# Fused attention and FFN: scratch weights stored by product and four features, half as many block moves, and a re-spaced plan

## The chip, the cores and the metric

The kernel runs on one core of a Trainium2 chip. The metric is the device time of one execution in microseconds. Engines: PE (matmul), PEld (its weight loads), DVE (vector), ACT (scalar), POOL (GpSimd), and SP, whose queue issues every DMA of this kernel.

## What is computed

Eight batches of 576 tokens; 8 heads of width 64. Heads 0 to 3 attend to the last 32 positions, heads 4 to 7 to every fourth of the last 128. The heads' outputs, put side by side, are the rows of x (4608 x 512), and a feed-forward layer follows:

```python
scores = np.where(masks[None], scale * np.matmul(q, k.transpose(0, 1, 3, 2)), -1e9)
attn = np.exp(scores - np.max(scores, -1, keepdims=True))
attn = attn / (np.sum(attn, -1, keepdims=True) + 1e-09)
x = np.matmul(attn, v)                     # then heads side by side: 4608 x 512
h = x @ w_in                               # 512 -> 2048
g = 0.5 * h * (1.0 + erf(h / sqrt(2)))
out = g @ w_out                            # 2048 -> 512
```

All in float32. A float32 operand of a large matmul is kept as a high and a low part of type fp32r, and a block takes three matmuls (high by high, low by high, high by low).

## The kernel before

**Tiling.** The 4608 tokens are nine chunks of 512; chunk 8 gathers the last 64 tokens of every batch. The eight heads of a chunk are four pairs p, treated two at a time as duos (p = 0 and p = 2). The feed-forward width is 16 features f of 128.

**Stages.** Chunks 0, 1 and 2 are computed densely: 192 matmuls of 128x128 by 128x512 for the hidden layer, 192 for the output. Chunks 3 to 8 go in three chunk pairs (`two_chunks`, line 1192), each layer as a two-by-two block product in seven products P1 to P7 (Winograd's form of Strassen), 672 matmuls a chunk pair. A *unit* is one product of one of eight features: six matmuls. The order of the units of a layer is a list: `first_units` (line 867), `second_units` (line 874).

**Scratch weights.** The products need sums of weight blocks. `prepare(layer, f, due)` (line 889), 16 calls in all, makes them while chunks 1 and 2 are computed: POOL adds high and low parts (line 906, two instructions), DVE forms four sums (line 914), ACT writes their high parts (line 926), DVE the low ones (line 929), and SP stores them to DRAM (`put`, line 931: four DMAs; `plain`, line 909: three DMAs straight from the weights). A unit's weights stand in `slabs` in the order of the unit list, four units of 1 MB a slab. `fetch` (line 1200) loads a slab into one of five ring tiles. Two unit tiles (`prep`) allow two preparations in flight.

**Attention beside it.** `attend` (line 1008) does a duo: a *scores visit* on PE (line 448), masked scores and minima on DVE, 16 exponentials on ACT (line 496), scaling and a transposition in 32x32 blocks on DVE (`turn`, line 523), moves of the turned blocks between partitions (`move`, line 1000), and a *values visit* on PE (line 577) for which the values v_sb must be loaded too. A duo's head pair takes eight moves of 32 KB:

```python
for r in range(4):
    for j in range(2):
        to = r // 2 * 2 + j
        nc.sync.dma_start(s.t[32 * to:32 * to + 32, r % 2], half[32 * r:32 * r + 32, j])
```

**Order of the work.** `Flow` (line 166) is a planner that runs when the program is built: jobs have an engine, a guessed time, due times and pool slots, and the planner fixes the order of the instructions of every engine; on the chip each engine and SP's queue works through its list in that order and waits where a semaphore says so. `pe` (line 825) puts a visit between matmuls when its time in PE's own clock has come, at least `VISITS` apart; the table `duos` (line 1435) holds those times, and `prepare` gets its due times in the loop at line 1450. Pools limit what may be in flight: 19 tiles of 1 MB (`w`), of which weights hold 16 until chunk 2 has used them, six PSUM banks for matmuls, two for visits, and three small tiles `go` for the hidden layer after gelu and for output copies.

Of the kernel before, what the change touches and what calls it, by code (L numbers as in the profile page):

```python
# [19 lines left out]
P = 128  # L20
# [145 lines left out]
class Flow:  # L166
# [4 lines left out]
    def __init__(self):  # L171
        self.busy, self.units, self.held, self.jobs, self.table = {}, {}, {}, [], ""

    def add(self, engine, time, do=None, after=(), due=0.0, begin=0.0, take=(), give=(), table="", land=0.0):
        j = dict(engine=engine, time=time, do=do, after=list(after), due=due, begin=begin, take=list(take), give=list(give),
                 table=table, land=land, ready=0.0, then=[])
        self.jobs.append(j)
        return j
# [15 lines left out]
    def run(self):  # L194
# [7 lines left out]
        while there:  # L202
# [14 lines left out]
            end = at + j["time"]  # L217
            self.table = j["table"] or self.table
            if e:
                self.busy[e] = end  # L220
            end += j["land"]
# [16 lines left out]
        assert n == len(self.jobs), (list(self.held), [(j["engine"], j["due"], j["take"]) for j in there if j["engine"] != "DMA"])  # L238
# [13 lines left out]
def attn_ffn(ctx: ExitStack, tc: tile.TileContext, qk, qk_lp, qk_ld, v, v_ld, w, outT):  # L252
# [270 lines left out]
    def turn(s):  # L523
        if s.wide:
            s.t = []
            for h in range(2):
                yield {"DVE": 0.5}
                t = work.tile([P, 3 * NU, KB], F32, tag="sm", name="turned", bufs=7)
                nc.vector.transpose(t.rearrange("p i b -> p (i b)"), s.sm[h].rearrange("p u k -> p (u k)"))
                s.t.append(t)  # L530
            return
        yield {"DVE": 0.62}
        s.t = work.tile([P, 2, 2 * NU, KB], F32, tag="sm", name="halves", bufs=7)
        nc.vector.transpose(s.t.rearrange("p j i b -> p i j b"), s.all.rearrange("p i (j b) -> p i j b", j=2))
# [303 lines left out]
    VISITS, WIDE_STEP, EXP_DUE = 5.0, 9.0, 5.0  # L838
# [28 lines left out]
    first_units = []  # L867
    for s in range(HALF):
        first_units += [(u, s - i) for i, u in enumerate((P1, P6, P7, P4)) if s >= i]
    first_units += [(P6, 7), (P7, 6), (P4, 5), (P5, 0), (P7, 7), (P4, 6), (P2, 0), (P5, 1), (P4, 7), (P2, 1), (P3, 0)]  # L870
    for f in range(2, HALF):
        first_units += [(P5, f), (P2, f), (P3, f - 1)]
    first_units.append((P3, HALF - 1))
# [3 lines left out]
    NSLAB = len(first_units) // 4  # L877
    place = [{u: i for i, u in enumerate(units)} for units in (first_units, second_units)]
    slabs = [scratch.tile([P, 4, 2, NW1], F32, name=f"slab{i}", tag=f"slab{i}") for i in range(2 * NSLAB)]

    def slab_at(layer, u, f):
        i = place[layer][u, f]
        return slabs[layer * NSLAB + i // 4][:, i % 4]

# [4 lines left out]
    def prepare(layer, f, due):  # L889
# [3 lines left out]
        names = (B11, B21, B12, B22) if layer == 0 else (B11, B12, B21, B22)  # L893
        at = {x: i for i, x in enumerate(names)}
        key = ("prepare", layer, f)
        cols = slice(layer * DM, (layer + 1) * DM)
        y = lambda x: st["q"][:, at[x], 1].bitcast(F32)
        weight = lambda x: weights[f if at[x] < 2 else g][:, :, layer * DM + at[x] % 2 * NW1:layer * DM + (at[x] % 2 + 1) * NW1]

        def add_up(i):  # L900
            def go():
                if i == 0:
                    st["q"] = wpool.tile([P, 4, 2, NW1], F32R, tag="w", name="units")
                x = weights[g if i else f].bitcast(F32)
                a, b = (x[:, k, cols].rearrange("p (i k) -> p i k", i=2) for k in range(2))
                nc.gpsimd.tensor_add(st["q"][:, 2 * i:2 * i + 2, 1].bitcast(F32), a, b)  # L906
# [12 lines left out]
        away = [flow.add("DMA", 2.0, plain, due=due, begin=due - 12, land=2.0)]  # L919
# [16 lines left out]
        away.append(flow.add("DMA", 2.7, put, [j], due + 1, land=2.0, give=[key]))  # L936
# [63 lines left out]
    def move(s):  # L1000

        half, s.t = s.t, work.tile([P, 2, 2 * NU, KB], F32, tag="sm", name="turned", bufs=7)
        for r in range(4):
            for j in range(2):
                to = r // 2 * 2 + j
                nc.sync.dma_start(s.t[32 * to:32 * to + 32, r % 2], half[32 * r:32 * r + 32, j])  # L1006

    def attend(c, p, scores_at, exps_at, values_at, lead=(14, 15)):
# [8 lines left out]
        def softmax_of(i, o, after, at, e):  # L1017
# [14 lines left out]
            else:  # L1032
                half = ("half",) + kk
                j = chain("DVE", [0.71], turn(o), [norms[-1]], e + 6 + 4 * step, step, take=[("sm", half)], give=[("sm",) + kk + (0,)])
                turns = [flow.add("DMA", 1.0, lambda: move(o), j, e + 6 + 5 * step, 0.0, turned, [half], land=2.2)]
# [3 lines left out]
        if wide:  # L1039
            for i, o in enumerate(pairs):  # L1040
                key = ("qk", c, o.p)
                q = flow.add("DMA", 2.6, load_qk(o, 1), due=scores_at[i] - 5, begin=scores_at[i] - lead[0], take=[("w", key)], land=2.0)
# [7 lines left out]
        else:  # L1050
            if c > 2:
                n = 2 if s.rest else 1
                keys = [("w", ("qk", c, p) + (i,) * i) for i in range(n)]
                q = [flow.add("DMA", 3.2 if s.rest else 2.6, load_qk(s, n), due=scores_at[0] - 5, begin=scores_at[0] - lead[0], take=keys, land=2.0)]
# [12 lines left out]
        if not wide:  # L1067
            key = ("v", c, p)
            vs = flow.add("DMA", 2.6, load_values(s), due=values_at - 6, begin=values_at - lead[1], take=[("w", key)], land=2.0)
# [26 lines left out]
        more = [("more", c, i) for i in range(2)]  # L1096
# [3 lines left out]
        for i, o in enumerate(pairs):  # L1100
            key = ("v", c, o.p)
            vs = flow.add("DMA", 2.0, load_values(o), due=values_at - 6 + i, begin=values_at - lead[1], take=[("w", key)], land=2.0)

            def run(o=o):
# [5 lines left out]
            def out(o=o):  # L1110
                c0 = o.p % 2 * P
                at_once(put_x(o, [ps[:, m, c0:c0 + P] for m in [6, 7] + [bank_of(x) for x in more]]))
            visit = flow.add("PE", 2.0, run, [turned[i], vs] + ([] if i else [turned[1]]),
                             take=[("upper", up)] + [("bank", x) for x in more] if not i else [],
                             give=[key] + [("turned", c, o.p, h) for h in range(2)])
            if i:
                visit["after"].append(puts[-1]["after"][0])
            visits.append((values_at + WIDE_STEP * i, visit))
            puts.append(flow.add("ACT", 1.7, out, [visit] + there[:1], values_at + WIDE_STEP * i + 4,
                                 take=[] if there else [("w", ("x",) + kx)]))  # L1120
            there.append(puts[-1])
        meet(puts, [up] + more)
# [23 lines left out]
    def chunk(c, parts):  # L1146
# [33 lines left out]
        for d in range(NC):  # L1180
# [7 lines left out]
            flow.add("DMA", 0.7, store, [k], clock[0] + 4 + d, give=[("o", c, d)], land=2.0)  # L1188
# [3 lines left out]
    def two_chunks(n):  # L1192
# [7 lines left out]
        def fetch(layer, i):  # L1200
            key = ("slab", n, layer, i)
# [3 lines left out]
            def go():  # L1205
                made[key] = wpool.tile([P, 4, 2, NW1], F32R, tag="w", name="ring")
                nc.sync.dma_start(made[key].rearrange("p m t k -> p (m t k)").bitcast(F32),
                                  slabs[layer * NSLAB + i].rearrange("p m t k -> p (m t k)"))
            units = (first_units, second_units)[layer][4 * i:4 * i + 4]
            after = {id(a): a for u, f in units for a in put_in[layer, u, f]}.values() if n == 0 else []  # L1210
            fetched[key] = flow.add("DMA", 2.6, go, list(after), clock[0] - 8, clock[0] - 25,
                                    take=[("w", key), ("ring", ("r",) + key)], land=2.0)
            return fetched[key]

        def weight(layer, u, f):
            i = place[layer][u, f]
            return (lambda: made["slab", n, layer, i // 4][:, i % 4]), fetch(layer, i // 4), \
                [("slab", n, layer, i // 4), ("r", "slab", n, layer, i // 4)] if i % 4 == 3 else []
# [119 lines left out]
        def keep_acc(name, bank, due, after=(), give=()):  # L1338

            jobs = []  # L1340
            for d in range(2):
# [4 lines left out]
                jobs.append(flow.add(("ACT", "DVE"), 0.6, go, [last[0]] + jobs + list(after), due + d, take=[("xg", ("acc", n, name))] if d == 0 else [],  # L1346
# [3 lines left out]
        def finish(name, bank, i, j, after, due, give=True, n_parts=1):  # L1350

            jobs, stores = [], []
            for d in range(2):
                for m in range(n_parts):
# [11 lines left out]
                    stores.append(flow.add("DMA", 0.7 / n_parts, store, [x], due + 2 + d, land=2.0))  # L1366
# [3 lines left out]
        evac2 = {}  # L1370
        for q, (u, f) in enumerate(second_units):
# [27 lines left out]
            def mm(u=u, f=f, w=w, b=b, begins=begins, key=key, ds=(0, 1)):  # L1399
# [6 lines left out]
            pe(6 * MM, mm, [got, second[u, f]] + before,  # L1406
               [("bank", (n, b, d)) for d in range(2)] if begins and f == 0 else [], slab_give + [key])
# [9 lines left out]
            elif u == P7:  # L1417
                j = keep_acc("u3", b, t)
                k = finish("p4", b, 1, 0, [last[0]] + evac2[P4], t + 1, give=False)
                meet(j + k, [(n, b, d) for d in range(2)])  # L1420
                evac2[P5] = finish("u3", "b", 1, 1, j, t, give=False)
            elif u == P2:
                finish("c1", b, 0, 0, [last[0]] + evac2[P1], t + 1)
            elif u == P3:
                finish("u2", b, 0, 1, [last[0]] + evac2[P6], t + 1, n_parts=2 if n == NPAIRS - 1 else 1)
# [3 lines left out]
    def visit_times(c, p, scores_at, exps_at, values_at, *more):  # L1429
# [5 lines left out]
    duos = [(2, 0, 2, (22.5, 27.5), 60), (2, 2, 8, (31, 36), 68), (3, 0, 14, (66, 71), CH + 6, (9, 12)),  # L1435
            (3, 2, 72, (75, 80), CH + 13, (9, 12)), (4, 0, CH + 18, (CH + 22.5, CH + 27.5), CH + 50, (9, 12)),
            (4, 2, CH + 24, (CH + 31, CH + 36), CH + 57, (9, 12))]
    for n in range(NPAIRS - 1):
        t, c = 2 * CH + n * PAIR, 5 + 2 * n
        duos += [(c, 0, t - 30, (t - 25, t - 20), t + 8), (c, 2, t + 1, (t + 3, t + 8), t + 22),  # L1440
                 (c + 1, 0, t + 10, (t + 13, t + 18), t + 36),
                 (c + 1, 2, t + 20, (t + 23, t + 28), t + 50) if c + 1 < LAST else
                 (c + 1, 2, (t + 18, t + 26), (t + 21, t + 29), t + 48)]
# [110 lines left out]
```

## Time and profile before

| | us |
|---|---|
| runs shown | 895.88 median of 3 (894.19 to 904.04) |
| the profiled execution | 896.98, of which the span of its instructions is 895.2 |
| granted TensorE clock, mean | 0.963 of full speed |
| busy | PE 837.5, PEld 688.4, DVE 596.3, ACT 469.7, POOL 56.5 |

A stretch of the trace is named by its start and end in microseconds. Chunk 0 with its weight loads runs to 136.7, chunks 1 and 2 to 383.6, the two chunk pairs with attention beside them to 662.6 (first layer of the second pair ended), the rest to 890.6, and the last additions and stores end at 895.2. Of each engine the rows give busy time, of SP the time that issuing took (SPq). A bracket behind an instruction is the idle time just before it on its engine and what ended it.

### The profile page before, as it was taken

How to read it: one execution, taken by the hardware profiler on the slowest of the kernel's cores; microseconds unless marked ns; L12 is line 12 of the kernel's file. 1: busy time of each engine (PE TensorE's matmuls, PEld its weight loads, DVE VectorE, ACT ScalarE, POOL GpSimd, SP SyncE). 2: the span in 40 equal slices, each digit the busy share in tenths (PEclk: the TensorE clock that was granted, in tenths of full speed). 3: DMA queues.
4: the chain of work that ended last, by engine and by line, in shares of the span. 5: the costliest groups of instructions: out<-in, count | busy, mean ns of one | idle time of the engine just before them, and what ended most of it. 6: DMA issues, size and time to landing. Idle time of an engine off the chain costs nothing.

```text
span 895.2 us, 19887 instructions
## 1 busy us (share of the span) xinstructions
PE 837.5 (94%) x8115; PEld 688.4 (77%) x8115; DVE 596.3 (67%) x950; ACT 469.7 (52%) x1187; POOL 56.5 (6%) x77
## 2 busy tenths in 40 slices
PE   7899999967886898998999999999899999999998
PEld 5778888846765786887888888787788888888886
DVE  6896977754874151657579677685597774389664
ACT  6786834552634263546565446555554443465441
POOL 5000012323240000000000000000000000000000
PEclk9799999988997898999999999899999999999999
DMA  9956127868977416276787546786855259655202
GB/s 372 416 219 266 48 94 250 273 203 245 328 233 223 180 32 252 93 268 218 247 348 293 191 182 230 239 297 236 349 203 199 98 199 386 261 192 194 85 0 95
DMA packets 60717, 195.55 MB, mean 218 GB/s; under 512 B 8274, under 2 KB 27730, under 8 KB 45394
## 3 DMA queue, kind: packets, MB, share of 16 engines
q1 hardware_dynamic: 60626, 194.28, 60.3%
q8 instruction: 64, 1.05, 0.5%
q14 instruction: 27, 0.22, 0.1%
HBM read 148.63 MB, written 38.80 MB: 209 GB/s over the span
## 4 chain that ended last, share of the span: by engine, by line
PE 68%; DMA 13%; SPq 8%; DVE 5%; issue 2%; ACT 2%; POOL 1%; DVEq 0%; ACTq 0%; POOLq 0%
PE ps L1402 25%; PE ps L1294 21%; SPq L1006 5%; PE ps L613 5%; PE ps L637 4%; PE ps L1175 4%; DMA ring<-slab 4%; DMA v_sb<-v 3%; DMA turned<-halves 2%; PE ps L1158 2%; PE ps L448 2%; PE ps L577 2%; DMA slab<-units 2%; DVE units L914 2%; SPq L933 2%
## 5 line engine op out<-in xcount | busy, mean ns | idle before, releaser
L1294 PE MATMUL ps<-parts,ring 128*128 128x512 f32 x1008 | 238.7, 397 | 2.6 <-issue 2.6
L1402 PE MATMUL ps<-parts,ring 128*128 128x512 f32 x1008 | 229.3, 389 | 0.0
L1294 PEld LDWEIGHTS ps<-parts,ring 128*128 128x128 f32 x1008 | 191.4, 191 | 43.8 <-issue 2.8
L1402 PEld LDWEIGHTS ps<-parts,ring 128*128 128x128 f32 x1008 | 189.2, 188 | 39.3
L1132 ACT CAST parts<-c 128x512 fp32r<-128x512 f32 x168 | 100.3, 621 | 71.4 <-DVE parts L1139 34.6
L1139 DVE TENSOR_TENSOR parts<-c,parts 128x512 fp32r<-128x512 f32 x168 | 112.3, 688 | 22.7 <-ACT parts L1132 21.4
L1158 PE MATMUL ps<-x,weight 128*128 128x512 f32 x384 | 97.1, 413 | 14.5 <-ACT gf L1163 14.5
L1158 PEld LDWEIGHTS ps<-x,weight 128*128 128x128 f32 x384 | 76.1, 201 | 31.7 <-ACT gf L1163 15.0
L1175 PE MATMUL ps<-parts,weight 128*128 128x512 f32 x384 | 89.0, 391 | 0.0
L274 DVE COPY c<-ps 128x512 f32<-128x512 f32 x62 | 42.2, 687 | 63.4 <-PE ps L1294 53.8
L1175 PEld LDWEIGHTS ps<-parts,weight 128*128 128x128 f32 x384 | 71.8, 188 | 15.2
L496 ACT ACTIVATE sm<-sm,st 128x64 f32<-128x64 f32 (+1 forms) x224 | 75.2, 339 | 15.7 <-DVE st L488 11.8
L1278 ACT ACTIVATE c<-c 128x512 f32<-128x512 f32 x96 | 58.3, 630 | 38.9 <-DVE c L1270 37.0
L1270 DVE TENSOR_TENSOR c<-c,ps 128x512 f32<-128x512 f32 x72 | 49.5, 688 | 27.1 <-PE ps L1294 24.0
L1328 DVE TENSOR_TENSOR c<-c 128x512 f32<-128x512 f32 x96 | 65.2, 687 | 1.1 <-ACT c L1278 0.6
L577 PE MATMUL ps<-turned,v_sb 64*64 64x32 f32 x1664 | 35.7, 237 | 25.5 <-DMA v_sb<-v 12.7
L906 POOL TENSOR_TENSOR units<-weight 128x512 f32<-128x512 f32 x32 | 44.9, 1428 | 208.3 <-DVE weight L368 112.2
L1139 DVE TENSOR_TENSOR parts<-gf,parts 128x512 fp32r<-128x512 f32 x32 | 23.7, 742 | 51.1 <-ACT parts L1132 51.0
L577 PEld LDWEIGHTS ps<-turned,v_sb 64*64 64x64 f32 x1664 | 33.3, 154 | 31.2 <-issue 14.1
L272 ACT COPY c<-ps 128x512 f32<-128x512 f32 x40 | 23.5, 586 | 61.2 <-PE ps L1294 57.7
L613 PE MATMUL ps<-x,weight 128*128 128x512 f32 x192 | 48.6, 404 | 0.0
L914 DVE TENSOR_TENSOR units<-units 128x256 f32<-128x256 f32 x64 | 37.9, 594 | 14.6 <-DMA turned<-halves 9.0
(93 smaller groups left out, 827.7 us busy)
## 6 DMA issues: line engine op xcount, KB each, us to landing
ring<-slab SPq DMA_DIRECT2D x84, 1024.0 KB, 5.9
v_sb<-v SPq DMA_DIRECT2D x17, 1024.0 KB, 6.4
raw_qk<-qk SPq DMA_DIRECT2D x32, 512.0 KB, 5.9
raw_w<-w SPq DMA_DIRECT2D x16, 1024.0 KB, 12.7
slab<-units SPq DMA_DIRECT2D x64, 256.0 KB, 4.3
slab<-weight SPq DMA_DIRECT2D x48, 256.0 KB, 4.5
turned<-halves SPq DMA_DIRECT2D x208, 32.0 KB, 3.0
mid_w<-w SPq DMA_DIRECT2D x4, 1023.5 KB, 16.8
```

The source lines that it names most:

```text
L496: nc.scalar.activation(t, s.sc[:, i // NU, at:at + 2 * KB] if s.c < 2 else t, AF.Exp, bias=s.st[:, 0, i:i + 1], scale=SCALE if s.c < 2 els ...
L577: nc.tensor.matmul(px(r)[h * D:(h + 1) * D, u * KB:(u + 1) * KB], s.v[rows, u, j, h * D:(h + 1) * D], s.t[rows, j, h * NU + slot(s, u)], s ...
L613: nc.tensor.matmul(bank, weights[f][:, t, cc * P:(cc + 1) * P], x[:, xx], start=n == 0, stop=n == 3 * NC - 1)
L914: return lambda: op(y(to), y(a), y(b))
L1132: nc.scalar.copy(to if len(x.shape) == 2 else to.rearrange("p (g i) -> p g i", i=32), x)
L1139: nc.vector.tensor_sub(a, x, b)
L1158: nc.tensor.matmul(bank, weights[f][:, i, cc * P:(cc + 1) * P], x[:, j], start=n == 0, stop=n == 3 * NC - 1)
L1175: nc.tensor.matmul(ps[:, bank_of(acc[d])], weights[f][:, i, DM + d * P:DM + (d + 1) * P], made["g", c, f][:, j], start=f == 0 and n == 0, ...
L1278: nc.scalar.activation(C[f][:, part], C[f][:, part], AF.Gelu)
L1294: nc.tensor.matmul(ps[:, bank_of(bank)], w()[:, a, i * P:(i + 1) * P], made[n, u, i][:, b], start=begins and k == 0, stop=k == 5, skip_gro ...
L1328: op(C[f][:, to], C[f][:, a], C[f][:, b])
L1402: nc.tensor.matmul(ps[:, bank_of((n, b, d))], w()[:, i, d * P:(d + 1) * P], made[key][:, j], start=begins and f == 0 and k == 0, stop=f == ...
```

## The change

1. The scratch weights are stored by layer, product and group of four features (`sums`, `both`, `one`). `put` is one DMA of 1 MB where it was four of 256 KB, `plain` two DMAs (512 and 256 KB) where it was three; a ring load takes one product's four features. Products in `both` are read in rows of 1 KB, the others in rows of 8 KB.
2. The units of the first layer go product by product over four features at a time, P1 P6 P7 P4 and then P5 P2 P3.
3. `turn` makes two transpositions: `half`, of the second half of each block alone, into a `go` tile, and all first halves twice into the tile that the values visit reads; four moves then overwrite half of that tile. The host lays out the values to fit.
4. `Flow` counts issue time apart from transfer time; `VISITS` is 7.0 for 5.0; the times of all visits and of the preparations are new; the wide values visits of chunk 8 no longer share one pair of banks.
5. In the last chunk pair the last product is computed for one half of the output rows and then for the other. Copies of accumulators wait for less.

```diff
-    VISITS, WIDE_STEP, EXP_DUE = 5.0, 9.0, 5.0
+    VISITS, WIDE_STEP, EXP_DUE = 7.0, 10.5, 5.0
...
-    for s in range(HALF):
-        first_units += [(u, s - i) for i, u in enumerate((P1, P6, P7, P4)) if s >= i]
...
+    four = [range(4), range(4, HALF)]
+    first_units = [(u, f) for fs in four for u in (P1, P6, P7, P4) for f in fs]
+    first_units += [(u, f) for fs in four for u in (P5, P2, P3) for f in fs]
...
+            drams["sums", layer, i] = scratch.tile([4, P, 4, 2 * NW1], F32, name=f"sums{layer}{i}", tag=f"sums{layer}{i}")
+            drams["both", layer, i] = scratch.tile([P, 8, 2 * NW1], F32, name=f"both{layer}{i}", tag=f"both{layer}{i}")
+            drams["one", layer, i] = scratch.tile([P, 8, NW1], F32, name=f"one{layer}{i}", tag=f"one{layer}{i}")
...
-            for u, x in ((P1, B11), (P2, B21), (P3, B22)):
-                nc.sync.dma_start(slab_at(layer, u, f), weight(x).bitcast(F32))
+            nc.sync.dma_start(drams["both", layer, half][:, f % 4 * 2:f % 4 * 2 + 2], weights[two][:, :, cols].bitcast(F32))
+            nc.sync.dma_start(drams["one", layer, half][:, f % 4 * 2:f % 4 * 2 + 2], weights[one][:, :, part].bitcast(F32))
...
-            for u, x in ((P6, B11), (P7, B22), (P4, B21), (P5, B12)):
-                nc.sync.dma_start(slab_at(layer, u, f), st["q"][:, at[x]].bitcast(F32))
+            nc.sync.dma_start(drams["sums", layer, half][:, :, f % 4].rearrange("u p k -> p u k"),
+                              st["q"].rearrange("p u t k -> p u (t k)").bitcast(F32))
...
-        nc.vector.transpose(s.t.rearrange("p j i b -> p i j b"), s.all.rearrange("p i (j b) -> p i j b", j=2))
+        s.half = work.tile([P, 2 * NU, KB], F32, tag="go", name="half", bufs=GO)
+        nc.vector.transpose(s.half, x[:, :, 1])
...
+        nc.vector.transpose(s.t, x[:, :, 0].unsqueeze(1).broadcast_to((P, 2, 2 * NU, KB)))
...
         for r in range(4):
-            for j in range(2):
-                to = r // 2 * 2 + j
-                nc.sync.dma_start(s.t[32 * to:32 * to + 32, r % 2], half[32 * r:32 * r + 32, j])
+            to = r ^ 1
+            nc.sync.dma_start(s.t[32 * to:32 * to + 32, r % 2], s.half[32 * r:32 * r + 32])
...
-    duos = [(2, 0, 2, (22.5, 27.5), 60), (2, 2, 8, (31, 36), 68), (3, 0, 14, (66, 71), CH + 6, (9, 12)),
+    duos = [(2, 0, 2, (22.5, 27.5), 57), (2, 2, 12, (31, 36), 77), (3, 0, 24, (66, 71), CH + 2, (9, 10)),
...
-        prepare(0, f, 14 + 12 * f)
-        prepare(1, f, 20 + 12 * f)
+        prepare(0, f, 14 + 8 * f)
+        prepare(1, f, 78 + 8 * f if f < 4 else CH + 52 + 7 * (f - 4))
```

**Where instructions move, SP's queue before the first values visit of chunk 2.** Before (L1006 moves, L933 and L911 stores of a preparation, L989 the values' load):

```order
L1006 DMA turned<-halves 32x256 x8
L933 DMA slab_1665<-units 128x512
L933 DMA slab_1667<-units 128x512
L933 DMA slab_1658<-units 128x512
L933 DMA slab_1663<-units 128x512
L911 DMA slab_1646<-weight 128x2x256
L911 DMA slab_1655<-weight 128x2x256
L911 DMA slab_1656<-weight 128x2x256
L1006 DMA turned<-halves 32x256 x8
L989 DMA v_sb<-v 128x2048
```

With the change (L1021 moves, L949, L927 and L928 the stores, L1006 the values' load):

```order
L1021 DMA turned<-half 32x256 x4
L949 DMA sums_1647<-units 128x4x512
L1021 DMA turned<-half 32x256 x4
L927 DMA both_1648<-weight 128x2x512
L928 DMA one_1649<-weight 128x2x256
L949 DMA sums_1647<-units 128x4x512
L1006 DMA v_sb<-v 128x2048
```

Between the moves of two head pairs stand one DMA or three of a preparation where seven stood, and the four moves are half the issues.

**ACT at the turn from exponentials to gelu.** Before, ahead of the second eight features of chunk 1 (L496 exponentials, L926 high parts of a preparation, L1163 gelu, L1132 its high part):

```order
L496 ACTIVATE sm,st<-sm,st 128x64 x9
L926 CAST units<-units 128x4x256
L496 ACTIVATE sm,st<-sm,st 128x64
L926 CAST units<-units 128x4x256
L1163 ACT_TABLE_LOAD
L1163 ACTIVATE gf<-ps 128x512
L1132 CAST parts<-gf 128x512
```

With the change, ahead of the second eight features of chunk 2 (L500, L943, L1177 and L1146 are the same four):

```order
L500 ACTIVATE sm,st<-sm,st 128x64 x10
L943 CAST units<-units 128x4x256
L500 ACTIVATE sm,st<-sm,st 128x64 x6
L943 CAST units<-units 128x4x256
L1177 ACT_TABLE_LOAD
L1177 ACTIVATE gf<-ps 128x512
L1146 CAST parts<-gf 128x512
```

The same pattern of high parts ahead of gelu stays in chunk 1, and comes to chunk 2, which had none, since four preparations are now due there.

## Rows read from the trace of the kernel before

**Rows 1.** Busy time by stretch: span, engines (instructions), granted clock, DMA share, GB/s.

```profile
136.70:383.60 246.90, 212.14 (x2434) 174.32 (x2433) 136.72 (x218) 116.20 (x335) 42.39 (x30) 0.92 0.65 211
383.60:662.60 279.00, 269.62 (x3186) 221.59 (x3185) 195.46 (x332) 155.76 (x434) 0.00 (x0) 0.98 0.70 257
662.60:890.60 228.00, 228.00 (x1007) 188.90 (x1006) 155.08 (x244) 102.77 (x174) 0.00 (x0) 1.00 0.46 173
```

**Rows 2.** PE's waits in 136.7 to 383.6: for whom, us in total, times, longest.

```profile
PE ps L1158 <- ACT gf L1163: 14.5, 2, 8.9
PE ps L577 <- DMA v_sb<-v: 12.7, 2, 8.6
PE ps L577 <- DMA turned<-halves: 3.3, 2, 2.8
PE ps L577 <- issue: 2.7, 2, 2.4
```

**Rows 3.** PE's waits in 383.6 to 662.6.

```profile
PE ps L577 <- DMA turned<-halves: 3.8, 6, 1.6
PE ps L577 <- issue: 2.9, 1, 2.9
```

**Rows 4.** Timeline of PE: start, duration, line, shapes, count, idle time before.

```profile
200.29 15.60 PE L1158 MATMUL ps<-x,weight 128*128 128x512 f32 x60 [8.92 <-ACT gf L1163]
...
275.23 3.74 PE L577 MATMUL ps<-turned,v_sb 64*64 64x32 f32 x128 [8.63 <-DMA v_sb<-v]
...
334.65 2.19 PE L577 MATMUL ps<-turned,v_sb 64*64 64x32 f32 x128
336.77 5.74 PE L1158 MATMUL ps<-x,weight 128*128 128x512 f32 x24
...
349.97 7.64 PE L1158 MATMUL ps<-x,weight 128*128 128x512 f32 x24
...
578.86 7.55 PE L1294 MATMUL ps<-parts,ring 128*128 128x512 f32 x24
```

**Rows 5.** Timeline of SP's queue: start, time to issue, line, transfer, count.

```profile
178.76 5.05 SPq L1006 DMA_DIRECT2D turned<-halves  x8
183.91 1.99 SPq L933 DMA_DIRECT2D slab<-units  x4
185.95 2.04 SPq L911 DMA_DIRECT2D slab<-weight  x3
...
209.87 6.75 SPq L1006 DMA_DIRECT2D turned<-halves  x8
```

**Rows 6.** DMA issues in 136.7 to 383.6: count, KB each, median us to landing.

```profile
slab<-units SPq DMA_DIRECT2D x64, 256.0 KB, 4.3
...
turned<-halves SPq DMA_DIRECT2D x111, 32.0 KB, 1.9
```

**Rows 7.** DMA issues in 383.6 to 662.6.

```profile
ring<-slab SPq DMA_DIRECT2D x47, 1024.0 KB, 8.3
...
turned<-halves SPq DMA_DIRECT2D x97, 32.0 KB, 4.9
```

**Rows 8.** Timeline of ACT in front of the longest wait.

```profile
197.28 1.04 ACT L926 CAST units<-units 128x1024 fp32r<-128x1024 f32 x1 [9.69 <-DMA slab<-units]
```

**Rows 9.** Groups by line: count, busy us, mean ns, idle before.

```profile
L906 POOL TENSOR_TENSOR units<-weight 128x512 f32<-128x512 f32 x32 | 44.9, 1428 | 208.3 <-DVE weight L368 112.2 <-DMA slab<-units 66.9 <-PE ps L448 17.6
...
L914 DVE TENSOR_TENSOR units<-units 128x256 f32<-128x256 f32 x63 | 37.5, 597 | 14.6 <-DMA turned<-halves 9.0 <-POOL units L906 4.2
...
L929 DVE TENSOR_TENSOR units<-units 128x1024 fp32r<-128x1024 f32 x16 | 21.3, 1332 | 3.3 <-ACT units L926 3.3
L534 DVE STREAM_TRANSPOSE halves<-sm 128x512 f32<-128x512 f32 x14 | 9.9, 708 | 12.7 <-DMA turned<-halves 12.5
...
L1270 DVE TENSOR_TENSOR c<-c,ps 128x512 f32<-128x512 f32 x72 | 49.5, 688 | 27.1 <-PE ps L1294 24.0
```

**Rows 10.** Timeline of DVE behind the last matmul.

```profile
890.59 1.43 DVE L1358 TENSOR_TENSOR u<-u,ps 128x256 f32<-128x256 f32 x4 [6.50 <-PE ps L1402]
```

More of the change, by code (lines that the diff above doesn't have):

```diff
@@ L171, in __init__, with add @@
     def __init__(self):
-        self.busy, self.units, self.held, self.jobs, self.table = {}, {}, {}, [], ""
-    def add(self, engine, time, do=None, after=(), due=0.0, begin=0.0, take=(), give=(), table="", land=0.0):
+        self.busy, self.units, self.held, self.jobs, self.table, self.wire = {}, {}, {}, [], "", 0.0
+    def add(self, engine, time, do=None, after=(), due=0.0, begin=0.0, take=(), give=(), table="", land=0.0, issue=0.5):
         j = dict(engine=engine, time=time, do=do, after=list(after), due=due, begin=begin, take=list(take), give=list(give),
-                 table=table, land=land, ready=0.0, then=[])
+                 table=table, land=land, issue=issue, ready=0.0, then=[])
         self.jobs.append(j)
@@ L217, in run @@
             end = at + j["time"]
+            if e == "DMA":
+                self.wire = max(self.wire, at + j["issue"]) + j["time"]
+                end = at + j["issue"]
             self.table = j["table"] or self.table
@@ L237, in run @@
                     there.append(k)
-        assert n == len(self.jobs), (list(self.held), [(j["engine"], j["due"], j["take"]) for j in there if j["engine"] != "DMA"])
+        assert n == len(self.jobs), (list(self.held), [(j["engine"], j["due"], j["take"]) for j in there if j["engine"] != "DMA" or j["due"] < 480])
 def at_once(gen):
@@ L1033, in softmax_of @@
                 half = ("half",) + kk
-                j = chain("DVE", [0.71], turn(o), [norms[-1]], e + 6 + 4 * step, step, take=[("sm", half)], give=[("sm",) + kk + (0,)])
-                turns = [flow.add("DMA", 1.0, lambda: move(o), j, e + 6 + 5 * step, 0.0, turned, [half], land=2.2)]
+                j = chain("DVE", [0.44, 0.71], turn(o), [norms[-1]], e + 6 + 4 * step, step, take=[("go", half)],
+                          give=[("sm",) + kk + (0,)])
+                j[1]["take"] += turned
+                turns = [flow.add("DMA", 0.4, lambda: move(o), j, e + 6 + 5 * step, 0.0, (), [half], land=2.2, issue=2.4)]
             return low[-2 if not wide else -1], turns[-1]
@@ L1095, in attend @@
             return
-        more = [("more", c, i) for i in range(2)]
         kx = ((c - 3) // 2, p // 2)
@@ L1101, in attend, with run @@
             key = ("v", c, o.p)
-            vs = flow.add("DMA", 2.0, load_values(o), due=values_at - 6 + i, begin=values_at - lead[1], take=[("w", key)], land=2.0)
-            def run(o=o):
+            more = [("more", o.p, k) for k in range(2)]
+            up = ("upper", c, o.p, 1)
+            vs = flow.add("DMA", 2.0, load_values(o), due=values_at - 6 + i, begin=values_at - lead[1], take=[("w", key)], land=2.3)
+            def run(o=o, more=more):
                 c0 = o.p % 2 * P
```

130 lines of the change are left out of this document (71 added, 59 removed).

## The prediction

> **What bounds the kernel now.** I read first the busy time by stretch [rows 1]. From 662.6 on PE is busy without a gap at full clock: 1007 matmuls in 228.0 us, 0.226 us each. Nothing can be gained there except a better order, and something can be lost. In chunks 1 and 2 PE is idle for 246.9 - 212.1 = 34.8 us and its mean granted clock is 0.92; in the next stretch it is idle for 279.0 - 269.6 = 9.4 us at 0.98. The question is what those two losses wait for.
>
> The waits of PE [rows 2] give names in chunks 1 and 2: 14.5 us for ACT's gelu, 12.7 us for the values v_sb, 3.3 us for moved blocks, 2.7 us "issue". In the next stretch [rows 3] it is moved blocks again, 3.8 us, and 2.9 us of issue in a values visit. All of these have SP's queue behind them. The gelu that PE waits for stands behind a high part of a preparation, and that instruction sat 9.69 us until a store of an earlier preparation had landed [rows 8]: the unit tile could not be filled again before. The timeline of SP [rows 5] shows the queue of that time: 5.05 us to issue eight moves, 1.99 and 2.04 us for the four and three stores of a preparation, 6.75 us for the next eight moves. A 256 KB store lands 4.3 us after its issue and a move 1.9 us [rows 6], so the time is spent ahead of the transfers. POOL, which begins each preparation, sat idle 66.9 us for stores to land [rows 9].
>
> After a gap PE also runs below full clock: 24 matmuls take 7.64 us behind the gap at 347 where the same 24 take 5.74 us at 336.77, and a values visit takes 3.74 us behind the 8.63 us gap where it takes 2.19 us at 334.65 [rows 4]. Seven such pieces in chunks 1 and 2 lose 0.3 to 2.3 us each, about 10 us together; two in the next stretch lose 1.8 us each (one is the 7.55 us row), about 4 us.
>
> **The change part by part.**
>
> *SP's issues.* Chunks 1 and 2 hold 16 preparations at 1.99 + 2.04 = 4.0 us, 64 us, and 14 head pairs of moves at 5.05 us or more, 71 us: 135 of 246.9 us, in bursts. After it the moves are half, 35 us. The large store has the descriptors of four small ones in one issue; no row has that form, so it costs between a quarter of 1.99 and all of it, 0.5 to 2.0 us. I take 1.2, the middle, since both ends are the same transfer counted in two ways. The two plain stores cost two thirds of 2.04, 1.4 us. So 16 x 2.6 = 42 us (30 to 54), and SP's total falls from 135 to 77 us (65 to 89).
>
> Here a rule of the Trainium skill speaks against the change. The rows say that eight moves hold SP for 5.05 to 6.75 us while one lands in 1.9 us [rows 5, 6]. The page "DMA: Bandwidth & Descriptors", section "Issuing engines are not separate DMA queues", says that the time a sequencer needs to initiate a DMA is usually small relative to the DMA itself. By the rule the saved issues would be worth nothing and the losses would stay; the trace has it the other way round for transfers of 32 KB, and I go by the rows.
>
> *The preparation's chain.* POOL 2 x 1.43, DVE 4 x 0.60, ACT 1.04, DVE 1.33 [rows 8, 9] are 7.6 us; the store follows. A 1 MB transfer lands between 4.3 us (the 256 KB store) and 8.3 us (the 1 MB ring load among heavy traffic) [rows 6, 7]; I take 6, between them, since traffic is thinner than in the second case. With 1.2 us of issue that is 14.8 us, and two unit tiles give one preparation per 7.4 us. The old due times asked for one every 6 us, which SP alone spent 4.0 us on; the new ones ask for one every 8, and put the last four far behind chunk 1. The cover is 0.6 us per preparation: thin, and gone if stores land in 8 us. What is late then is ACT's high part, with gelu queued behind it.
>
> *The second transposition* adds half to one 708 ns transposition [rows 9] for each of 26 head pairs, 0.35 to 0.71 us of DVE. DVE is busy 136.7 of 246.9 and 195.5 of 279.0 us [rows 1], and 2.5 us of issues less stand behind it. On the path: nothing, as long as a visit's data is early by more than 0.7 us.
>
> *The `go` tiles.* `half` holds one of three until its four moves have landed, and gelu and output copies need the same three. For the second eight features of chunk 2 I followed the orders with the rows' durations: four head pairs' halves come just ahead of the first gelu there, which must wait for a tile until moves issued some 5 us earlier land. PE has two PSUM banks of 12 matmuls, 2.7 us each, to go on with, and then waits about 2 us. Elsewhere gelu finds a tile. Cost: 2 us.
>
> *Visits.* With the new spacing I followed SP's queue by hand. Before visits of the later duos of chunks 2 to 4, blocks, values and keys are there 1 to 4 us before PE; in the two chunk pairs over 5 us before. Where the margin is that thin, a landing at the longer end (8.3 for 6 us) makes PE wait. I count three such misses at 2.2 us, the mean between the rows' 1.6 and 2.8 [rows 2, 3], each followed by 1.8 us of slow clock: 3 x 4 = 12 us. Ends: none, 0; six, 24.
>
> *Order by fours.* A unit is 6 x 0.226 = 1.36 us. P2 of feature f + 2 takes the bank of P2 of f, which DVE frees in 0.688 us [rows 9] while the unit between them runs: cover 0.67 us. If DVE is late by an instruction there, four units per chunk pair wait up to 0.69 us, 3 x 4 x 0.69 = 8 us. In order DVE has that addition next, so I take 0 and keep 8 as an end.
>
> *Rows of 1 KB in `both`.* 24 ring loads of 84; each may take up to twice the 8.3 us, against a ring in which a tile lasts 4 x 1.36 = 5.4 us and up to five are ahead. Hidden; 0.
>
> *The last product by halves.* DVE's 1.43 us of additions behind the last matmul [rows 10] become half: -0.7 us. The other parts (copies, wide visits) cost nothing that waits.
>
> **The sum.** The profiled execution took 896.98 us. All losses gone: 34.8 + 10 + 9.4 + 4 + 0.7 = 59, giving 838. The median of the runs is 1.1 us lower: 837. Put back 2 + 12 = 14: **851 us**.
>
> **The rivals.**
>
> *The preparations still bind.* POOL, DVE, ACT and landing, not issue, set the pace. For it: 7.6 us of the chain is engine time, and its cover is 0.6 us. Against it: before, POOL waited for stores, 66.9 us. Then the 14.5 us for gelu and 12.7 us for values stay, with some 8 us of clock: 837 + 35 = **872** (862 to 886).
>
> *Issues were not the cause.* SP has slack between its bursts, and it is the transfers that come late: the DMA engines are busy 0.65 of chunks 1 and 2 [rows 1]. The bytes are unchanged, so the waits stay, less what the spacing gives: 886 to 905, about **895**. Against it stand bursts of 5 us in which SP only issues [rows 5], so 0.07. The quoted rule of the Trainium skill's page "DMA: Bandwidth & Descriptors" would make this the likeliest case.
>
> *Slower: the `go` tiles.* Seven duos of halves are turned in chunks 1 and 2, and DVE waited up to 12.5 us in all for moves to free tiles [rows 9]. If two halves of a duo sit there as halves did before (turned, then behind a preparation's store in SP's queue and eight issues: about 10 us), gelu has one tile left, PE has 5.4 us of banks, and each duo costs (10 - 5.4) + 2 of clock, 46 us for seven; at 14 us, 74. Then 837 + 14 + 46 to 74 = 897 to 925, about **911**. It decides when halves sit longer than 10 us; with four issues of 0.63 us and 1.9 to 4.9 us to land [rows 5 to 7] I expect 4.5 to 7.5 us.
>
> **How the numbers follow.** The forecast's own case, 837 to 862, has 0.64; the preparations 0.20; issues not the cause 0.07; `go` 0.09. The range 837 to 882 leaves out the two last and the top of the second, 0.19; its low end is all losses gone. Differences within 1% (9 us) are what a measurement here can't tell from none. Faster by more than that: 0.64 + 0.20 - 0.01 = 0.83; same 0.07; slower 0.10, the `go` case and a little for the fours.
>
> **What would show it.** Right: in the two stretches PE's idle time falls from 44 to about 10 us with the clock at 0.97 or more; the wait for gelu is under 4 us; four moves take SP about 2.5 us; POOL waits less for stores. The ends of chunk 2 and of the first layer of the second pair come some 40 and 50 us earlier. Wrong: PE waits for gelu with ACT's high part before it (preparations), or for gelu with moves of `half` before it (`go`), or for the vector engine inside the first layer of the last pair, which had no gap (fours).

## The result, and the profile after

The changed kernel takes **843.59 us** (median of 4 runs, 842.75 to 846.21), the kernel before 897.12 us beside it (894.19 to 904.04): a ratio of 0.9398, 95% interval 0.9339 to 0.9457. The forecast was 851 us, range 837 to 882. The profiled execution took 843.32 us, its span 841.5 us, at a mean granted clock of 0.987.

Busy time by stretch, the same three stages as in [rows 1] (span, PE, PEld, DVE, ACT, POOL, granted clock, DMA share, GB/s):

```profile
135.57:348.10 212.53, 205.63 (x2562) 168.52 (x2560) 141.66 (x230) 120.07 (x353) 44.77 (x30) 0.98 0.71 247
348.10:604.73 256.63, 255.52 (x2674) 210.43 (x2673) 193.91 (x332) 153.42 (x392) 0.00 (x0) 1.00 0.71 256
604.73:837.00 232.27, 232.27 (x1390) 192.45 (x1389) 157.36 (x248) 113.22 (x211) 0.00 (x0) 1.00 0.51 180
```

PE's idle time in the first two stretches fell from 34.8 + 9.4 to 6.9 + 1.1 us, and the clock rose from 0.92 and 0.98 to 0.98 and 1.00. Between the two kernels some visits changed stage: chunk 2 now holds one more scores visit, the last stretch two wide values visits.

All that PE waits for in these stretches (for whom: us in total, times, longest), against [rows 2, 3]:

```profile
PE ps L1172 <- ACT gf L1177: 6.9, 2, 4.1
PE ps L1307 <- DVE c L1283: 0.8, 1, 0.8
PE ps L585 <- issue: 0.3, 1, 0.3
```

No visit waits for values or for moved blocks. SP's queue around the start of chunk 1's second eight features (start, time to issue, line, transfer, count), the place of [rows 5]:

```profile
175.98 2.54 SPq L1021 DMA_DIRECT2D turned<-half  x4
178.56 0.58 SPq L927 DMA_DIRECT2D both<-weight  x1
179.19 0.47 SPq L928 DMA_DIRECT2D one<-weight  x1
179.76 2.77 SPq L1021 DMA_DIRECT2D turned<-half  x4
182.70 0.46 SPq L949 DMA_DIRECT2D sums<-units  x1
184.44 2.71 SPq L1021 DMA_DIRECT2D turned<-half  x4
...
189.26 0.78 SPq L1006 DMA_DIRECT2D v_sb<-v  x1
190.14 3.92 SPq L1021 DMA_DIRECT2D turned<-half  x4
```

Before, three head pairs' moves and the stores between them ran from 178.76 to 202.7, 23.9 us (the third's take 5.14 us from 197.55); now they run from 175.98 to 187.15, 11.2 us, and the 1 MB store of a preparation is issued in 0.46 us. Summed over chunks 1 and 2, the rows of SP's queue hold 180.0 us of issuing before (111 moves 81.0, 112 stores 77.4) and 95.2 us now (52 moves 41.1, 48 stores 31.4).

The 6.9 us that are left stand where ACT turns from exponentials to gelu. ACT, chunk 1 and then chunk 2 (the bracket is the idle time before and what ended it):

```profile
189.37 1.04 ACT L943 CAST units<-units 128x1024 fp32r<-128x1024 f32 x1 [4.69 <-DVE units L931]
190.43 1.28 ACT L1177 ACT_TABLE_LOAD   x1
191.72 0.60 ACT L1177 ACTIVATE gf<-ps 128x512 f32<-128x512 f32 x1
...
296.68 1.04 ACT L943 CAST units<-units 128x1024 fp32r<-128x1024 f32 x1 [2.27 <-PE ps L1172]
298.52 1.28 ACT L1177 ACT_TABLE_LOAD   x1 [0.80 <-DMA turned<-half]
299.81 0.60 ACT L1177 ACTIVATE gf<-ps 128x512 f32<-128x512 f32 x1
```

and PE at the same two places:

```profile
192.37 11.26 PE L1172 MATMUL ps<-x,weight 128*128 128x512 f32 x36 [2.77 <-ACT gf L1177]
...
300.46 4.60 PE L1172 MATMUL ps<-x,weight 128*128 128x512 f32 x12 [4.13 <-ACT gf L1177]
```

In both cases the high part of a preparation stands ahead of the table load and waits for the vector engine's sums. Those of the first stood in DVE's order behind two head pairs' turning, one's scaling and the low part of an earlier preparation. The row of the second names a matmul, but its sums, too, end just before it starts. DVE, the sums of the first and of the second:

```profile
187.44 1.77 DVE L931 TENSOR_TENSOR units<-units 128x256 f32<-128x256 f32 x4
...
294.73 1.79 DVE L931 TENSOR_TENSOR units<-units 128x256 f32<-128x256 f32 x4
```

Only 0.80 us is a wait for moves to free a `go` tile.

### The profile page after: what moved, and what is told of

Same layout as the page of the kernel before. It is cut to its first block, busy times and chain, and to the rows that moved or that the text cites. A ratio compares the mean times of both kernels' runs of the same rounds, so it can differ in the third digit from the quotient of the medians.

```text
span 841.5 us, 19621 instructions
## 1 busy us (share of the span) xinstructions
PE 819.0 (97%) x8115; PEld 672.9 (80%) x8115; DVE 601.2 (71%) x964; ACT 481.9 (57%) x1201; POOL 59.0 (7%) x77
## 4 chain that ended last, share of the span: by engine, by line
PE 85%; DVE 7%; ACT 3%; issue 2%; DMA 1%; SPq 0%; DVEq 0%; ACTq 0%
PE ps L1415 27%; PE ps L1307 27%; PE ps L1172 9%; PE ps L1189 6%; PE ps L645 5%; PE ps L621 4%; PE ps L585 3%; PE ps L452 2%; DVE units L931 2%; DVE units L946 1%; DMA raw_qk<-qk 1%; PE ps L564 1%; PE ps L797 1%; DVE sm L486 1%; ACT sm L500 1%
## 5 line engine op out<-in xcount | busy, mean ns | idle before, releaser
L1307 PE MATMUL ps<-parts,ring 128*128 128x512 f32 x1008 | 232.9, 391 | 0.8 <-DVE c L1283 0.8
L1415 PE MATMUL ps<-parts,ring 128*128 128x512 f32 x1008 | 230.1, 390 | 0.0
L1146 ACT CAST parts<-c 128x512 fp32r<-128x512 f32 x168 | 102.5, 622 | 77.1 <-DVE parts L1153 47.9
L1172 PE MATMUL ps<-x,weight 128*128 128x512 f32 x384 | 94.8, 406 | 6.9 <-ACT gf L1177 6.9
L500 ACT ACTIVATE sm<-sm,st 128x64 f32<-128x64 f32 (+1 forms) x224 | 75.4, 339 | 15.9 <-DVE st L492 15.8
L278 DVE COPY c<-ps 128x512 f32<-128x512 f32 x57 | 39.3, 690 | 58.1 <-PE ps L1307 50.8
L276 ACT COPY c<-ps 128x512 f32<-128x512 f32 x45 | 26.5, 588 | 68.2 <-PE ps L1307 62.5
L921 POOL TENSOR_TENSOR units<-weight 128x512 f32<-128x512 f32 x32 | 47.3, 1501 | 222.4 <-DVE weight L372 110.9
L621 PE MATMUL ps<-x,weight 128*128 128x512 f32 x192 | 46.8, 393 | 0.0
L645 PE MATMUL ps<-g,weight 128*128 128x512 f32 x192 | 46.3, 391 | 0.5 <-DVE g L640 0.5
L645 PEld LDWEIGHTS ps<-g,weight 128*128 128x128 f32 x192 | 35.9, 188 | 8.3 <-DVE g L640 0.9
L500 ACT ACTIVATION_READ_ACCUMULATOR sm<-sm,st 128x1 f32 x224 | 42.3, 189 | 0.0
```

The costliest lines, as they stand in the source:

```text
L500: nc.scalar.activation(t, s.sc[:, i // NU, at:at + 2 * KB] if s.c < 2 else t, AF.Exp, bias=s.st[:, 0, i:i + 1], scale=SCALE if s.c < 2 els ...
L621: nc.tensor.matmul(bank, weights[f][:, t, cc * P:(cc + 1) * P], x[:, xx], start=n == 0, stop=n == 3 * NC - 1)
L645: nc.tensor.matmul(ps[:, d], weights[f][:, t, DM + d * P:DM + (d + 1) * P], gs[f][:, u], start=f == 0 and n == 0, stop=f == NF - 1 and n == 2)
L1146: nc.scalar.copy(to if len(x.shape) == 2 else to.rearrange("p (g i) -> p g i", i=32), x)
L1172: nc.tensor.matmul(bank, weights[f][:, i, cc * P:(cc + 1) * P], x[:, j], start=n == 0, stop=n == 3 * NC - 1)
L1307: nc.tensor.matmul(ps[:, bank_of(bank)], w()[:, a, i * P:(i + 1) * P], made[n, u, i][:, b], start=begins and k == 0, stop=k == 5, skip_gro ...
```

## The experiments

Two theories stood against each other: SP's time to issue had made the waits ("issues"), or the times in the plan had ("times"). Medians are of runs beside runs of the kernel before; ratios are to those. Differences in us are between medians, and between sets of runs the median of the kernel before itself moved from 897.1 to 899.7 us.

**Issues undone, plan kept.** Three kernels issue the same bytes in the changed kernel's order, with more DMAs:

```diff
# stores: four and three DMAs for one and two
+            for u in range(4):
+                nc.sync.dma_start(drams["sums", layer, half][u, :, f % 4], st["q"][:, u]...)
+            for j in range(2):
+                nc.sync.dma_start(drams["both", ...][:, f % 4 * 2:f % 4 * 2 + 2, j * NW1:(j + 1) * NW1], ...)
# moves: eight of 16 KB for four of 32 KB
+            for i in range(2):
+                n = slice(i * NU, (i + 1) * NU)
+                nc.sync.dma_start(s.t[32 * to:32 * to + 32, r % 2, n], s.half[32 * r:32 * r + 32, n])
```

Stores alone. 

> The changed kernel, a preparation's stores as four DMAs of 256 KB and three of 256 KB in place of one of 1 MB, one of 512 KB and one of 256 KB; the order of the work as it is. Theory 'issues': some 2.7 us more of SP for each preparation, 850 to 865 us; from then on the high part of the last preparation ahead of a gelu comes later, the wait for gelu over 10 us. Rival 'times': 843 to 846 us.

Measured: 847.99 us, ratio 0.9430 (0.9394 to 0.9467); 4.4 us above the change, between the ranges of the two theories. The two ratios' intervals overlap, so that these 4.4 us are not clear of noise, and the sign failed: PE waits 6.6 us for gelu, not over 10.

Moves alone. 

> The changed kernel, each of the four moves of a head pair issued as two DMAs of 16 KB; the order of the work and the bytes as they are. Theory 'issues': 2.5 us more of SP for each of 26 head pairs, halves sit longer in their go tiles, 850 to 868 us. Rival 'times': 843 to 846 us.

Measured: 870.30 us, 0.9689 (0.9645 to 0.9732); 26.7 us above, 2 us over the range of "issues".

Both. 

> The changed kernel and its plan, but each preparation's stores go out as four and three DMAs again and each head pair's moves as eight (of 16 KB): the number of issues of before, the order of the changed kernel. Theory 'issues' (SP's time to issue made the waits): SP's issuing in chunks 1 and 2 grows by some 2.7 us for each of 16 preparations and 2.5 us for each of 14 head pairs, about 78 us, PE waits for gelu and v_sb again, 870 to 890 us. Rival 'times' (the re-spaced visits and preparations made the gain): PE finds its data all the same, 844 to 852 us.

Measured: 880.60 us, 0.9794 (0.9759 to 0.9829); 37.0 us above, as "issues" expected. PE's longest waits in it, chunks 1 and 2, to hold against [rows 2]:

```profile
PE ps L1177 <- ACT gf L1182: 14.6, 2, 9.4
PE ps L585 <- DMA v_sb<-v: 9.6, 2, 7.0
PE ps L585 <- issue: 4.7, 1, 4.7
```

The totals are back nearly as they were, with the new plan in place, but the waits for gelu are not the old ones. Before, both were in chunk 1, at 200.29 [rows 4], behind a high part that waited for a store [rows 8], and at

```profile
223.48 5.01 PE L1158 MATMUL ps<-x,weight 128*128 128x512 f32 x12 [5.57 <-ACT gf L1163]
```

With the old number of issues the one in chunk 1 stands behind a high part that waits 4.68 us for the vector engine's sums, as in the changed kernel, and the longer one is in chunk 2, where ACT's table load waits 6.1 us for moves to free a `go` tile (PE's timeline, then ACT's waits from 136 to 400 us):

```profile
331.40 5.00 PE L1177 MATMUL ps<-x,weight 128*128 128x512 f32 x12 [9.45 <-ACT gf L1182]
...
ACT L1182 <- DMA turned<-half: 6.7, 2, 6.1
```

That tie of gelu to the moves exists only in the changed kernel; before, `halves` stood in tiles of another pool (`sm`). So part of the 37.0 us is what issues cost the changed kernel, not what they had cost the kernel before. The same holds for eight moves alone, whose table load waits 5.8 us there.

With eight moves alone, SP's queue at the place shown above reads:

```profile
176.82 5.07 SPq L1023 DMA_DIRECT2D turned<-half  x8
181.94 0.58 SPq L927 DMA_DIRECT2D both<-weight  x1
182.56 0.47 SPq L928 DMA_DIRECT2D one<-weight  x1
183.13 5.31 SPq L1023 DMA_DIRECT2D turned<-half  x8
188.54 0.53 SPq L949 DMA_DIRECT2D sums<-units  x1
189.17 5.90 SPq L1023 DMA_DIRECT2D turned<-half  x8
...
197.18 0.77 SPq L1006 DMA_DIRECT2D v_sb<-v  x1
```

The first moves begin 0.8 us later than in the changed kernel, and the values' load is issued 7.9 us later. Eight moves of 16 KB take SP what eight of 32 KB took [rows 5]: the price goes by the issue, not by the byte. Nor do the transfers land later, though there are twice as many: a move lands in 1.9 us here (2.8 in the changed kernel), and the DMA share of chunks 1 and 2 is 0.65 against 0.71.

**Times undone, issues kept.** The tables `duos`, `VISITS` and the preparations' due times of before in the changed kernel, and the new ones in the kernel before:

```diff
-    VISITS, WIDE_STEP, EXP_DUE = 7.0, 10.5, 5.0
+    VISITS, WIDE_STEP, EXP_DUE = 5.0, 9.0, 5.0
...
-        prepare(0, f, 14 + 8 * f)
-        prepare(1, f, 78 + 8 * f if f < 4 else CH + 52 + 7 * (f - 4))
+        prepare(0, f, 14 + 12 * f)
+        prepare(1, f, 20 + 12 * f)
```

> The changed kernel with the table of visits, the spacing (5.0 and 9.0) and the preparations' due times of before; few issues, four moves. Theory 'issues': most of the gain stays, 845 to 860 us. Rival 'times': most of it goes, 875 to 897 us, with PE waiting for gelu behind a preparation's high part in chunk 1 as before.

Measured: 844.84 us, 0.9394 (0.9359 to 0.9429): nothing lost (1.2 us, within noise).

> The kernel before with nothing changed but the table of visits, the spacing (7.0 and 10.5) and the preparations' due times, which are those of the change. Theory 'issues': SP's queue is as loaded as before, PE still waits for gelu and v_sb some 20 us, 880 to 897 us. Rival 'times': 850 to 870 us.

Measured: 892.87 us, 0.9943 (0.9909 to 0.9976). The two largest of PE's waits over the whole run:

```profile
PE ps L577 <- DMA v_sb<-v: 12.2, 3, 7.7
PE ps L1158 <- ACT gf L1163: 8.6, 1, 8.6
```

So by itself the re-spacing is worth about 5 us on the old queue and none on the new one. "Times" falls. (The order that `Flow` gives the queue, change 4, was not undone by itself.)

**The moves alone in the kernel before** (its scratch layout, stores and times kept; the two transpositions, `move` and the values' layout as in the diff of the change).

> The kernel before with the change of the moves alone: two transpositions, four moves of 32 KB for a head pair, the values laid out to fit; scratch weights, stores, order and times of before. Theory 'the moves' issues are the larger part' (eight of them on SP cost the changed kernel 27 us): 866 to 876 us. Rival 'the queue stays full' (seven stores a preparation, one preparation due every 6 us, still fill SP): 880 to 895 us. If halves in go tiles make gelu wait: 895 us or more.

Measured: 867.04 us, 0.9654 (0.9604 to 0.9705): 30.2 us, 0.56 of the change's gain, from the moves, as expected. PE still waits 9.4 us for gelu and 3.8 us for v_sb there. This run also halves the moved bytes; the eight moves of 16 KB, which keep the bytes, cost the changed kernel 26.7 us, its `go` tiles' part included.

**Another queue.** `nc.sync` became `nc.gpsimd` in `move`, with eight moves and with four.

> The changed kernel with eight moves of 16 KB for each head pair, as in the run with eight moves on SP that took 870.3 us, but issued by POOL, which otherwise only adds for the preparations. Theory 'SP's time to issue': PE finds v_sb and keys again, 842 to 852 us. Rival 'the transfers themselves' (their number and size, whoever issues them): 865 to 873 us. Third: POOL stands waiting for a transposition with a preparation's addition behind it, and PE waits for gelu behind that preparation's high part, 852 to 875 us.

Measured: 1199.64 us, 1.3351 (1.3289 to 1.3413).

> The changed kernel with its four moves of a head pair issued by POOL in place of SP; SP's issuing falls by some 2.5 to 3.9 us for each head pair. If SP still sets anything in chunks 1 and 2: 836 to 841 us. If what is left is the vector engine's sums ahead of the high part (6.9 us of waiting for gelu): 841 to 845 us. If POOL's waits delay the preparations: 848 to 860 us.

Measured: 999.42 us, 1.1143 (1.1081 to 1.1204). All three expectations missed for both: POOL takes far longer from one move to the next than SP. Its timeline with four moves, one row a move:

```profile
202.43 0.51 POOL L1021 DMA_DIRECT2D turned<-half  x1 [1.51 <-issue]
204.47 0.51 POOL L1021 DMA_DIRECT2D turned<-half  x1 [1.54 <-issue]
206.49 0.50 POOL L1021 DMA_DIRECT2D turned<-half  x1 [1.51 <-issue]
```

A move comes every 2.0 us, 0.51 us of it shown as the instruction. Halves sit in `go` tiles meanwhile, and ACT's table load ahead of gelu waits for one:

```profile
ACT L1177 <- DMA turned<-half: 26.4, 1, 26.4
ACT gf L1177 <- DMA turned<-half: 16.7, 3, 6.7
```

PE waits 61.1 us for gelu. These two runs don't tell SP's time from the number of transfers, as they were meant to; they show the slower rival of the prediction (the `go` tiles) at work once a move takes about three times as long to issue.

**Is it the `go` tiles with eight moves on SP?** Halves in one tile of their own:

```diff
-        s.half = work.tile([P, 2 * NU, KB], F32, tag="go", name="half", bufs=GO)
+        s.half = work.tile([P, 2 * NU, KB], F32, tag="half", name="half", bufs=1)
```

> The kernel with eight moves of 16 KB (870.3 us), its halves in a tile of their own, one at a time, in place of a go tile; gelu and the output copies keep all three. If the price of the eight moves comes through go tiles held until the moves have landed: 846 to 856 us, with no wait of gelu or of an output copy for a move. If it comes through SP's lateness itself (keys, values, stores): 864 to 876 us.

Measured: 880.53 us, 0.9796 (0.9737 to 0.9855), more than the 870.3 us it was to mend and outside both ranges. PE's wait for gelu fell to 6.2 us from 11.6, but DVE now stood for that one tile (136 to 400 us):

```profile
DVE half L539 <- DMA turned<-half: 42.0, 10, 8.4
```

Inconclusive: room was left for one tile only, and it is a worse neck than three shared ones.

**Wide visits sharing banks again.** `more` and `up` taken once for both visits, the second visit behind the first, and given back after both copies, as before.

> The changed kernel, the two wide values visits of chunk 8 sharing one pair of banks again as before. If unsharing cost and gave nothing: 842 to 845 us. If it took away the idle 2.6 us and slow clock behind a wide visit in the second chunk pair of before: 846 to 850 us, with a gap behind the first wide visit.

Measured: 846.55 us, 0.9422 (0.9366 to 0.9478). Its second layer of the second pair:

```profile
619.00 2.08 PE L577 MATMUL ps<-turned,v_wide 32*64 32x32 f32 x189
623.44 0.42 PE L577 MATMUL ps<-turned,v_wide 32*64 32x32 f32 x3 [2.35 <-issue]
623.79 11.22 PE L1418 MATMUL ps<-parts,ring 128*128 128x512 f32 x36
```

In the changed kernel no gap stands there, and 36 matmuls of this shape behind a shorter gap read:

```profile
596.43 8.46 PE L1307 MATMUL ps<-parts,ring 128*128 128x512 f32 x36 [0.80 <-DVE c L1283]
```

The granted clock of the slower 36 is 0.73, of the others 1.00. A gap of 2.35 us and 2.76 us of slow clock make 5 us in this trace, which is of the slowest of the four runs (849.42 us). The medians lie 3 us apart, inside the range expected, but the intervals of the ratios overlap: the trace shows what the unsharing removes, the times alone do not.

**A version that beats both.** Only the preparations' due times change, so that none falls due just ahead of a second eight features:

```diff
-        prepare(0, f, 14 + 8 * f)
-        prepare(1, f, 78 + 8 * f if f < 4 else CH + 52 + 7 * (f - 4))
+        prepare(0, f, 14 + 8 * f if f < 6 else 68 + 8 * (f - 6))
+        prepare(1, f, 84 + 8 * f if f < 4 else CH + (46, 53, 83, 90)[f - 4])
```

> The changed kernel with other due times of the preparations alone: none is due in the last 12 us before the second eight features of chunk 1 or of chunk 2. If a high part that waits for the vector engine's sums ahead of gelu makes the 6.9 us that PE still waits there: 834 to 840 us, the wait for gelu under 2 us. If the exponentials alone bring gelu that late, or the preparations moved back delay the first ring loads of the first chunk pair: 841 to 848 us.

Measured: **832.03 us**, 0.9260 (0.9222 to 0.9298), 2 us under the range of the first case; PE does not wait for gelu at all. By stretch:

```profile
136.00:337.48 201.48, 201.48 (x2565) 166.14 (x2565) 135.25 (x229) 119.02 (x341) 45.76 (x30) 1.00 0.76 263
337.48:593.57 256.09, 255.29 (x2674) 209.94 (x2672) 192.34 (x332) 155.09 (x406) 0.00 (x0) 1.00 0.71 255
593.57:826.70 233.13, 233.13 (x1393) 192.91 (x1391) 155.91 (x247) 112.60 (x213) 0.00 (x0) 1.00 0.51 180
```

Chunks 1 and 2 run without a gap at full clock. In chunk 2 no high part stands between the exponentials and gelu any more; in chunk 1 one still does, at 184.27 where it stood at 189.37.

The same times with the old number of issues:

> The kernel with other due times of the preparations (832.0 us), its stores as four and three DMAs and its moves as eight again. If those times need the short queue: 866 to 880 us, about as far above 832 us as the 37 us that the old issues cost the changed kernel. If with no preparation due ahead of gelu the issues no longer matter: 834 to 850 us.

Measured: 881.33 us, 0.9833 (0.9763 to 0.9903): 49 us above, no better than with the other times (880.60), and 1 us over the range of the first case. PE waits 16.2 us for v_sb in it. These due times are worth 11.6 us with the short queue and nothing with the long one.

## Why the prediction was right, and where its sizes were not

**The cause was right, of the moves above all.** Issues undone cost 37.0 us of the 53.5 with the plan kept, times undone cost nothing, and the moves alone gave the kernel before 30.2 us. "Issues were not the cause" (0.07) falls. For the moves the rule quoted from the Trainium skill's page "DMA: Bandwidth & Descriptors" does not hold in this kernel: a move takes SP 0.73 to 0.80 us on average and lands in 1.9 to 2.8 us, so its issue is not small beside its landing. Nor is it "the other way round", as the prediction had it by holding eight issues against one landing. For a 1 MB store, 0.57 us to issue and 6.1 to land, the rows agree with the page.

The prediction set out from a high part that waited 9.69 us for a store [rows 8], and counted the stores' issues like the moves'. No run shows this part: the stores' issues undone cost 4.4 us, within noise, and with all issues undone the waits for gelu have other causes (above).

**SP's total.** 135 us were counted before for moves and stores, from single bursts; all rows together hold 158. After, 77 (65 to 89) were forecast and 72.5 found, but by two errors that offset each other: moves 41.1 for 35 (four take 3.2 us on average, not 2.5), stores 31.4 for 42. The large store was put between 0.5 and 2.0 us, taken at 1.2: 16 took 9.1 us, 0.57 each. The two plain stores were put at 1.4 us and took 1.4.

**The losses.** The idle time, 44.2 us, was read off. The clock's share, 14 us, was too small: the version at full clock has 689.9 us of PE's busy time over the same work, the kernel before 709.8 [rows 1], so about 20 us, if all of the difference is clock. Only the pieces visibly slow in the timeline had been counted. Taking all losses out would have given 831 us rather than 837, which is where the version of 832.03 us stands.

**What was put back.** This term failed in its parts. Visits: three misses of 4 us, 12 us, were expected; one of 0.3 us came. Gelu: 2 us for `go` tiles ahead of chunk 2's second eight features were expected; the place was right, but 4.13 us came, of which 0.80 us is the `go` tile, and 2.77 us in chunk 1 that were not forecast. The cause is a rival of the prediction, the preparations' chain, in small: high parts waiting for the vector engine's sums. So the sign "wait for gelu under 4 us" failed with 6.9. Idle 8.0 us and 4.4 us of slow clock (694.3 us of PE's busy time up to the last matmul against 689.9) make 12.4 in place of 14. With 6 us from the clock's share that is about the 7.4 us between 851 and 843.6. That the total put back came out near is luck: the visits' 12 us did not come, and waits for gelu that were not forecast took their place.

**The preparations still bind (872 us).** Not as a pace: POOL's wait for stores to land fell from 66.9 us [rows 9] to

```profile
POOL units L921 <- DMA sums<-units: 34.6, 6, 9.2
```

and a 1 MB store lands in 6.1 us (6 were taken); with all old issues that wait is 68.3 us again. Moving due times alone, with the chain as it is, brought 11.6 us, so it was the place of a high part in ACT's order, not the chain's length.

**The other terms.** The order by fours was taken at nothing, with 8 us as an end: PE waited once, 0.8 us, for DVE inside the first layer (596.43, shown above). Ring loads of `both` in rows of 1 KB land in 8.1 us in the second stretch, the others in 6.5 to 8.8, and PE waits for none; "up to twice" had no row behind it. The transposition of the first halves takes 0.67 us and that of `half` 0.44, 0.40 us more than the one before, and no visit waits for them. The wide visits were put among parts that "cost nothing that waits"; unsharing them removes a gap of some 3 to 5 us with its slow clock, which the forecast had counted under the losses of the second stretch without saying what would remove them. Behind the last matmul 1.43 us of additions [rows 10] became

```profile
837.94 0.75 DVE L1371 TENSOR_TENSOR u<-u,ps 128x256 f32<-128x256 f32 x2 [4.69 <-PE ps L1415]
```

0.7 us less, as forecast. Chunk 2 ended 35.5 us earlier (40 forecast), the first layer of the second pair 57.9 us (50), of which some 4 us are the two wide visits that now lie behind it.

**What stays open.** The moves' eight issues cost 26.7 us for 46 us more of SP's time in chunks 1 and 2 (141.4 against 95.2), the stores' cost 4.4 us for 33 us more (128.1). That moves stand right ahead of the values' load and hold `go` tiles, while a store has a second unit tile as cover, fits both. The traces show both ways at work with eight moves alone: in chunks 1 and 2 PE waits 5.7 us for v_sb and 8.4 us for the gelu behind a `go` tile, where the changed kernel has no wait for v_sb and one of 4.1 us for that gelu. How the 26.7 us divide stays open, since the run that was to separate the `go` tiles did not. Eight moves also double the number of transfers; the landing times speak against that as the cause, but no run keeps SP's time and changes the number alone. And 880.6 us with all old issues is still 16 to 19 us under the kernel before: new times (5), wide visits (3 to 5), the halved bytes of the moves and the queue's order are candidates, the last two not tried by themselves.

## What to carry to other kernels

Sum the time that the one issuing queue takes, not only what each transfer takes: a queue in bursts delays what stands behind the burst. Then ask what does stand behind each burst, since the sum alone is not the price: 46 us more of issuing cost 26.7 us in moves, 33 us more cost 4.4 in stores. Change the number of issues first and the plan afterwards: with the long queue no table of due times brought more than 5 us, with the short one a table alone brought 11.6 us. Price slow clock from a gap-free stretch of the same work, not from the pieces that look slow.

## What was not expected of the hardware

What an issue costs SP does not go by its bytes: 0.73 us a move of 32 KB before, 0.80 us a move of 16 KB, 0.66 us a store of 256 KB, 0.57 us a store of 1 MB (sums of the rows by their counts); the values' loads of 1 MB took 0.44 us each before and 0.79 in the changed kernel. The same move issued by POOL comes every 2.0 us and made the kernel 155.8 us slower with four moves a head pair, 356 us with eight.
